# Starting the exit code of VectorE and ScalarE on a fetch-block boundary, in a group-norm kernel bound by DMA

## Chip, cores, metric

One NeuronCore of a Trainium2 chip. The metric is the device time in microseconds (us) of one execution. An execution's *span*, from the first to the last of the program's own instructions, is recorded beside it. The time was about 2 us more than the span in every run (1.79 to 2.02 us in the means of the kernels); this difference, called *time minus span* below, is what this study turned out to be about. Spans are recorded to 0.1 us.

## The reference

```python
# x: (128, 1024, 32, 16) bf16; 32 groups of 32 channels x 512 pixels = 16384 values
xr = x.reshape(B, G, C // G, H, W)
mu = xr.mean(axis=(2, 3, 4), keepdims=True)
var = ((xr - mu) ** 2).mean(axis=(2, 3, 4), keepdims=True)
xn = (xr - mu) / jnp.sqrt(var + 1e-5)
return xn.reshape(B, C, H, W) * g[None, :, None, None] + b[None, :, None, None]
```

134 MB are read and 134 MB written.

## The kernel before

The input is cut into 32 pieces of 4 MB, each 128 partitions (4 samples x 32 groups) by 16384 values. A ring of six pieces lies in SBUF. TensorE and VectorE add up a piece, ScalarE squares it and takes the root, VectorE scales it in place, and SyncE issues loads and stores. ScalarE, TensorE and VectorE each run a loop on their own; the loop body stands in the program once (VectorE's closing branch, one source line, runs 32 times in the trace).

```python
def in_rounds(e, one, ahead=None):          # ScalarE, TensorE
    with nc.Fori(0, ROUNDS, 1, engines=[e.engine]) as t:
        more = (t, ahead(t)) if ahead else (t,)
        for c in range(REST):
            one(c, *more)
        with e.If(t < ROUNDS - 1):
            for c in range(REST, SLOTS):
                one(c, *more)

def on_vector(e):
    ...
    with nc.Fori(1, NT + 1, 1, engines=[e.engine]) as i:
        ...
        for k, a in enumerate(parts):       # 32 channels of a piece
            ts = e.tensor_scalar(
                out=a, in0=a, scalar1=scl[:, k : k + 1], scalar2=bia[:, k : k + 1],
                op0=ALU.mult, op1=ALU.add,
            )
            if (k + 1) % KQ == 0:
                ts.then_inc(done, 1)

def on_sync(e):
    ...                                     # all loads and stores of pieces
    e.wait_ge(s_fin, 16 * sum(store_parts(i) for i in range(NT - SLOTS, NT)))
```

When an engine leaves its loop, the *exit code* follows: on each engine a few drains and semaphore waits that form a closing barrier over all five engines (VectorE's first drain lasts 3.7 us, until its last scaling ends). Behind the barrier the trace names no instructions, but the device time of the profiled run, 630.24 us, is 2.0 us more than its span.

## Time and profile before

| | before |
|---|---|
| device time, median of the first 3 runs | 630.41 us (629.87 to 630.49) |
| span of the profiled run | 628.2 us |
| bytes moved, mean rate over the span | 268.44 MB, 427 GB/s |
| VectorE, ScalarE busy | 79%, 80% |
| last ScalarE, last VectorE arithmetic ends | 603.0, 614.3 us |
| last store lands, SyncE's wait ends | 627.6 us |

How to read it: the DMA engines are full until 622.5 us (busy share 1.00 from 620 to 622.5 us, 0.20 in the 2 us after), so the compute engines have slack, and everything that ScalarE and VectorE do after 603 and 614 us lies beside the last stores until 627.6 us. The busy times in part 1 of the page (us, share of the span, instructions):

```profile
PE 180.9 (29%) x513; PEld 0.2 (0%) x2; DVE 495.8 (79%) x1185; ACT 503.0 (80%) x258; POOL 1.0 (0%) x8
```

No compute engine is full. The prediction shows the other lines.

### The profile page before, as it was taken

To read this page: it belongs to the slowest core of one execution; us is meant where nothing else is said; L and a number is where in the kernel's file an instruction comes from. 1 tells how busy PE (TensorE), PEld (TensorE's weight loads), DVE (VectorE), ACT (ScalarE), POOL (GpSimd) and SP (SyncE) were. 2 spreads that over 40 slices of the span, in tenths; PEclk is the share of its full clock that TensorE was granted. 3 is DMA by queue.
4 is the path that set the end of the run, shared out by engine and by line. 5 is a ranking of instruction groups with operands and counts; after the bars stand their busy time and mean duration, and the time that the engine had idled before them with its cause. 6 is when DMAs were issued, how large, how long until landed. Compare 5 with 4: busy or idle time off the path is not lost.

```text
span 628.2 us, 2492 instructions
## 1 busy us (share of the span) xinstructions
PE 180.9 (29%) x513; PEld 0.2 (0%) x2; DVE 495.8 (79%) x1185; ACT 503.0 (80%) x258; POOL 1.0 (0%) x8
## 2 busy tenths in 40 slices
PE   2633334330244402333023330333303333063000
PEld 0000000000000000000000000000000000000000
DVE  1479999999298982999729997299973999799961
ACT  0899999999389992999919999199990999979930
POOL 0000000000000000000000000000000000000000
PEclk9776776675586655877558775577755776577555
DMA  9999999999999999999999999999999999999996
GB/s 401 434 434 401 434 434 434 434 434 434 432 434 434 434 434 434 432 432 430 434 434 434 432 426 434 434 432 432 434 430 432 430 432 434 432 432 434 434 434 275
DMA packets 9888, 268.44 MB, mean 427 GB/s; under 512 B 1184, under 2 KB 1184, under 8 KB 1184
## 3 DMA queue, kind: packets, MB, share of 16 engines
q1 hardware_dynamic: 9792, 268.44, 99.3%
q10 hardware_dynamic: 96, 0.00, 0.0%
HBM read 134.22 MB, written 134.22 MB: 427 GB/s over the span
## 4 chain that ended last, share of the span: by engine, by line
DMA 35%; ACT 35%; DVE 21%; PE 4%; issue 1%; DVEq 1%; SPq 0%; ACTq 0%
ACT ja L269 32%; DMA ring<-in_x_dram 23%; DVE ring L336 15%; DMA out_dram<-ring 11%; DVE jp L306 5%; PE ps L218 4%; DMA gb_b<-in_b_dram 2%; ACT jm L261 2%; ACT var L279 1%; ACT std L283 1%; DVEq L320 1%; DVE bia L330 0%; DVE scl L326 0%; DVE rstd L324 0%; SPq L170 0%
## 5 line engine op out<-in xcount | busy, mean ns | idle before, releaser
L269 ACT ACTIVATE ja<-ring,nm 128x8192 fp8e5<-128x8192 bf16 x64 | 455.8, 7122 | 2.1
L336 DVE TENSOR_SCALAR ring<-ring,scl,bia x1024 | 333.6, 407 | 1.2
L218 PE MATMUL ps<-ring,eye 128*128 128x512 bf16 x512 | 180.6, 525 | 394.0 <-DVE jp L306 227.3
L306 DVE SCALAR_TENSOR_TENSOR jp<-ring 128x4096 fp8e5 (+1 forms) x32 | 141.4, 4420 | 75.7 <-PE ps L218 75.7
L261 ACT ACTIVATE jm<-ps 128x513 fp8e5<-128x513 f32 x32 | 19.1, 597 | 94.1 <-PE ps L218 94.0
L324 DVE RECIPROCAL rstd<-std 128x1 f32 x32 | 5.5, 171 | 26.8 <-ACT std L283 25.8
L269 ACT ACTIVATION_READ_ACCUMULATOR ja<-ring,nm 128x1 f32 x64 | 11.9, 186 | 0.0
L279 ACT ACTIVATE var<-sq,eps_t 128x1 f32<-128x1 f32 x32 | 9.4, 295 | 1.0
L283 ACT ACTIVATE std<-sq,var 128x1 f32<-128x1 f32 x32 | 9.4, 294 | 1.0
L312 DVE COPY gb<-gb_p 128x64 f32<-128x64 f32 x1 | 0.2, 224 | 12.6 <-PE gb_p L213 12.6
L330 DVE SCALAR_TENSOR_TENSOR bia<-scl,nm,gb 128x32 f32<-128x32 f32 x32 | 8.0, 251 | 1.1
L326 DVE TENSOR_SCALAR scl<-gb,rstd 128x32 f32<-128x32 f32 x32 | 7.7, 241 | 1.1
L261 ACT ACTIVATION_READ_ACCUMULATOR jm<-ps 128x1 f32 x32 | 6.2, 194 | 0.0
L306 DVE DVE_READ_ACCUMULATOR jp<-ring (+1 forms) x32 | 4.5, 141 | 0.0
L213 PE MATMUL gb_p<-gb_b,rep 32*128 32x64 bf16 x1 | 0.2, 205 | 12.3 <-DMA gb_b<-in_b_dram 12.3
L257 ACT ACT_TABLE_LOAD x1 | 1.3, 1283 | 1.8 <-PEq L369 1.8
L194 POOL TENSOR_SCALAR_AFFINE_SELECT rep<-ones_b 32x128 bf16<-32x128 bf16 x1 | 0.3, 303 | 0.0
L190 POOL TENSOR_SCALAR_AFFINE_SELECT eye<-ones_b 128x128 bf16<-128x128 bf16 x1 | 0.3, 292 | 0.2 <-issue 0.2
L257 ACT ACTIVATE warm<-eps_t 128x1 f32<-128x1 f32 x1 | 0.2, 202 | 0.0
L186 POOL MEMSET ones_b<- 128x128 bf16 x1 | 0.2, 204 | 0.3 <-POOLq L369 0.3
L215 PEld LDWEIGHTS <-eye 128*128 128x128 bf16 x1 | 0.1, 105 | 0.1
L213 PEld LDWEIGHTS gb_p<-gb_b,rep 32*128 32x128 bf16 x1 | 0.1, 100 | 12.3 <-issue 12.3
(5 smaller groups left out, 0.5 us busy)
## 6 DMA issues: line engine op xcount, KB each, us to landing
ring<-in_x_dram SPq DMA_DIRECT2D x32, 4096.0 KB, 37.3
out_dram<-ring SPq DMA_DIRECT2D x30, 4096.0 KB, 27.8
out_dram<-ring SPq DMA_DIRECT2D x2, 2048.0 KB, 12.9
out_dram<-ring SPq DMA_DIRECT2D x4, 1024.0 KB, 11.4
gb_b<-in_g_dram ACTq DMA_DIRECT2D x1, 2.0 KB, 7.7
gb_b<-in_b_dram ACTq DMA_DIRECT2D x1, 2.0 KB, 11.0
```

Of the source, the lines that this page charges most:

```text
L218: return e.add_instruction(mybir.InstMatmult(name=nc.get_next_instruction_name(), engine=e.engine, start_tensor_calc=(k == 0), stop_tensor ...
L257: e.activation(out=warm[:], in_=eps_t[:], func=ACT.Sqrt)
L261: e.activation(out=jm[:], in_=sums_and_pairs(c), func=ACT.Identity, scale=-inv_n, accum_out=nm[:, place(c) : place(c) + 1], saturate=False ...
L269: e.activation(out=ja[:], in_=slot(c)[:, h * (F // 2) : (h + 1) * (F // 2)], func=ACT.Square, bias=nm[:, place(c) : place(c) + 1], scale=1 ...
L279: e.activation(out=var[:], in_=sq[:, 0:1], func=ACT.Identity, bias=eps_t[:], scale=inv_n).then_inc(varred[c], 1)
L283: e.activation(out=std[:, place(c) : place(c) + 1], in_=sq[:, 1:2], func=ACT.Sqrt, bias=var[:], scale=inv_n).then_inc(stded, 1)
L306: e.scalar_tensor_tensor(out=jp[:], in0=aps[0], scalar=1.0, in1=aps[1], op0=ALU.mult, op1=ALU.add, accum_out=aps[2], saturate=False,).then ...
L320: e.keepalive_nop([e.lower_ap(a) for a in (*parts, nm_i, std_i, *ahead)])
L324: e.reciprocal(out=rstd[:], in_=std_i).then_inc(inverted, 1)
L326: e.tensor_scalar(out=scl[:], in0=gb[:, 0:KC], scalar1=rstd[:], scalar2=None, op0=ALU.mult).then_inc(scaled, 1)
L330: e.scalar_tensor_tensor(out=bia[:], in0=scl[:], scalar=nm_i, in1=gb[:, KC : 2 * KC], op0=ALU.mult, op1=ALU.add,).then_inc(shifted, 1)
L336: ts = e.tensor_scalar(out=a, in0=a, scalar1=scl[:, k : k + 1], scalar2=bia[:, k : k + 1], op0=ALU.mult, op1=ALU.add,)
```

## The change

The intent: the exit code is to start a block of 128 instructions of its own, in the hope that what follows it is then fetched while the engine idles beside the last stores, not after the closing barrier. The block of 128 is the change's premise. The traces show instruction packets of 8192 bytes (in the kernel before at 629.54 and 630.04 us), not how many instructions these hold. A *slot* is an instruction's place in its block, counted from 0. The loader leaves a gap behind the loop and puts a branch over it (in the changed kernel 38 ns on ScalarE, 47 ns on VectorE). This is the whole diff:

```diff
+FETCH = 128
@@
+    def enter_exit(e):
+
+        e.addr_align(FETCH, max_nops=0)
+
@@ on_scalar
         in_rounds(e, one)
+        enter_exit(e)
@@ on_vector
                     ts.then_inc(done, 1)
+        enter_exit(e)
```

## The prediction

> **What bounds the kernel now.** I read the page first, because it says whether any engine is full. Parts 1 to 3 do, and the two lines below from part 2 and part 3 carry it.
>
> ```profile
> DMA  9999999999999999999999999999999999999996
> GB/s 401 434 434 401 434 434 434 434 434 434 432 434 434 434 434 434 432 432 430 434 434 434 432 426 434 434 432 432 434 430 432 430 432 434 432 432 434 434 434 275
> ...
> q1 hardware_dynamic: 9792, 268.44, 99.3%
> ```
>
> The 16 DMA engines are at nine tenths or more in every slice but the last, at a flat 434 GB/s. 268.44 MB at 434 GB/s is 618.5 us, so about 98% of the 628.2 us span is moving each byte in once and out once. VectorE is busy 79% and ScalarE 80%, so neither sets the pace. The chain of part 4 walks through ScalarE squares and VectorE scaling, but only because a store waits for them; with the queue never empty, that chain isn't the bound. No change of VectorE or ScalarE code inside the loop should move the middle of the run. What can move is the last slice.
>
> Second, the timeline of the last 29 us, since the change touches only code behind the loops.
>
> ```profile
> 602.74 0.29 ACT L283 ACTIVATE std<-sq,var 128x1 f32<-128x1 f32 x1
> 603.07 0.16 DVE L324 RECIPROCAL rstd<-std 128x1 f32 x1 [5.10 <-ACT std L283]
> ...
> 603.83 10.42 DVE L336 TENSOR_SCALAR ring<-ring,scl,bia  x32
> 606.54 8.08 SPq L170 DMA_DIRECT2D out_dram<-ring  x4
> ```
>
> ScalarE's last activation ends at 603.03 us, VectorE's last at 603.83 + 10.42 = 614.25, and the last store is issued by 614.62. From there only DMA works: 13.6 us until the span ends at 628.2. The waits of the store queue say so too:
>
> ```profile
> SPq L183 <- DMA out_dram<-ring: 12.9, 1, 12.9
> ```
>
> This is the kernel's one wait for its last stores: 12.9 us long. ScalarE stands about 24.5 us and VectorE about 13 us at the closing barrier.
>
> Third, the exit code itself: the instructions of the closing barrier, which the profile lists under one line of the launch code.
>
> ```profile
> L380 ACTq DRAIN  x2: 8/12/15, 603.1 to 627.9; - x2
> L380 DVEq DRAIN  x2: 19/1868/3717, 610.6 to 628.0; - x2
> L380 SPq EVENT_SEMAPHORE  x2: 17/17/17, 627.9 to 628.2; - x2
> L380 ACTq EVENT_SEMAPHORE  x2: 17/17/17, 627.9 to 628.2; - x2
> L380 DVEq EVENT_SEMAPHORE  x2: 21/21/21, 627.9 to 628.2; - x2
> ```
>
> The exit code per engine is short: two drains and two semaphore waits. ScalarE reaches its first drain at 603.1 us, 0.1 us after leaving its loop, VectorE at 610.6 us (its sequencer is ahead of its arithmetic by ten queued operations). Neither shows a stall on entering the exit, so in the kernel before the exit code was already in instruction memory. The last two waits end at 628.2: that is the end of the span.
>
> Fourth, the DMA view of stretches that the page leaves out: 628 to 632 us, after the kernel's own code.
>
> ```profile
> DMA packets 2, 0.02 MB, mean 4 GB/s; under 512 B 0, under 2 KB 0, under 8 KB 0
> ...
> q14 instruction: 2, 0.02, 1.1%
> ```
>
> Two packets of the instruction kind, 8192 bytes each, start at 629.54 and 630.04 us in the trace and take 0.31 and 0.40 us. The same view of 0 to 628 us has queues 1 and 10 alone, so no instructions at all were fetched while the kernel ran. [...] So right after the closing barrier somebody runs into code that isn't there. Also, the profiled run took 630.24 us by the device's count and its span is 628.2: 2.0 us of the count lie outside the span, and these fetches end at 629.85 and 630.44, 1.6 and 2.2 us behind it.
>
> [...] the VectorE compare-and-branch at the loop's end took 50 ns here[...].
>
> **The change, part by part.** It adds one alignment mark behind each of the two loops, with no padding executed: the loader leaves a gap and branches over it. (1) Added: one branch per engine, 0.05 us, at 603.0 and 610.5 us. Both lie beside the stores; on the path to the end: 0. (2) Moved: [...] I expect the two packets of 629.5 and 630.0 to move to about 603 and 611 us. If the fetch is a cold one, the time is some 1.3 us (end of the code, 628.2, to the first packet, 629.5) plus 0.3 to 0.4 us of packet, say 1.7 us idle; between stores I allow three times that, 5 us. ScalarE has 24.5 us to spare and VectorE, which needs nothing new before 627.9, 17 us from 610.6. VectorE's ten queued operations run on meanwhile. On the path: 0. (3) Added to the stores' DMA: two packets of 8 KB among 268 MB. On one DMA engine each costs 0.3 to 0.4 us. The end is set by the slowest of 16 engines: in the trace 15 of the last 16 completions land by 625.1 and the last at 627.56. Only if a fetch falls on that one engine does the end move, by up to 0.4 each; 1 in 16 if spread evenly. Expected: under 0.05 us. (4) Removed: the wait after 628.2. If the two engines stall there for their code, the count holds up to 1.7 to 2.2 us of it[...]. I take 0.5 to 1 us as what must remain, hence a gain of 1.0 to 1.5 us where the fetch is inside the count. Sum where it is: 630.4 - 1.25 = 629.2. Sum where it isn't: 630.4.
>
> **The rivals.** First, the fetches are outside the count or are mere prefetches that nobody waits for. For it: the second one ends at 630.44, later than 630.24, and a prefetch would look the same; against it: two packets match the two engines that the author picked, and a start of the count some tenths before the first instruction would be enough to explain the 630.24. It makes 630.4, no change. I give it 40%. Second, the fetch collides with the last stores, on the engine that lags by 2.4 us, or slows VectorE before it has issued its last scaling. For it: the DMA engines are full until 622.5 us; against it: 16 KB only, and the queued VectorE work. It makes 630.7 to 631.2; 7%. Third, the marks shift the loops[...]: at 1.7 us for each of 31 VectorE back edges that is 53 us of VectorE time, of which its 21% of idle time (132 us) could hide most, but late stores would make 640 and more. Against it: the marks stand behind the loops, and the loop bodies (VectorE 48 recorded instructions, ScalarE eight per sample and six samples) are short; 1%. The main view, a real gain of about 1.25 us, has the remaining 52%.
>
> **Range and chances.** 0.52 x 629.2 + 0.40 x 630.4 + 0.07 x 630.9 + 0.01 x 640 = 629.9; I lean to the likeliest case and put 629.6. The three runs of before spread over 0.62 us, so I widen the two main cases by 0.5 either way and cut at the bottom for a gain of nearly 2 us: 628.4 to 630.9. Two per cent would be 12.6 us, six times all that lies outside the span, and nothing in the loop changes: faster by 2% 0.005, slower by 2% 0.01, within 0.985.
>
> **What would show each step.** Right: instruction packets of 8 KB inside the span near 603 and 611 us, none or fewer after 628; a span that stays at 628.2 within 0.5 us; ScalarE's and VectorE's first drain up to 5 us later than 603.1 and 610.6; count minus span down from 2.0 to 0.5 to 1.0 us. If the packets move and count minus span stays at 2.0, the first rival holds. If the span grows with the last store's completion later, the second. If instruction packets appear all through the span, the third. If the packets stay at 629.5 and 630.0, they belonged to other engines, and step (2) is wrong.

What the prediction told of the hardware and no trace or run of this case showed is cut from it, and the cuts are marked: a paragraph of rules and figures for instruction fetches and branches (the 50 ns of VectorE's compare-and-branch stay, from the trace), the size of an instruction, the reason given in step (2) for the packets to move, the reason given in step (4) for a rest that must remain, and in the third rival how a back edge would come to fetch. The sum came to 630.4 - 1.25 = 629.2 us where the fetch is inside the count and 630.4 where it isn't, and weighted with the rivals to 629.9, put as 629.6. The 0.5 to 1 us that must remain was from no measured number. The third rival's 53 us, 31 times 1.7, assumed a back edge that fetches anew in each turn, which had not been shown.

## The result

The changed kernel took 630.41 us (median of 6 runs, 630.14 to 630.97), the kernel before 630.40 us (6 runs). The ratio is 1.0003, 95% interval 0.999 to 1.0016: the same. Ratios here are the mean time of one kernel's fast runs over that of the other's of the same rounds, so not quite the ratio of the medians.

The span of the profiled run is 628.2 us, as before. The DMA part of the page of the changed kernel:

```profile
GB/s 401 432 434 403 434 434 434 434 434 432 434 434 432 434 430 432 434 432 434 434 434 434 434 434 430 432 432 428 434 432 434 430 430 430 432 426 434 434 435 286
DMA packets 9890, 268.46 MB, mean 427 GB/s; under 512 B 1184, under 2 KB 1184, under 8 KB 1184
...
q14 instruction: 2, 0.02, 0.0%
```

The rates are those of before. New is the row of queue 14: two instruction packets inside the span. In the trace they start at 607.80 and 615.51 us. The wait of SyncE for the last stores, and the exit code (one source line, by engine and kind: shortest/median/longest in ns, then the first and last start in us):

```profile
SPq L185 <- DMA out_dram<-ring: 12.4, 1, 12.4
```

```profile
L388 ACTq DRAIN  x2: 8/48/88, 604.0 to 627.9; - x2
L388 DVEq DRAIN  x2: 19/1605/3191, 611.6 to 627.9; - x2
L388 SPq EVENT_SEMAPHORE  x2: 17/17/17, 627.8 to 628.1; - x2
L388 ACTq EVENT_SEMAPHORE  x2: 17/17/17, 627.8 to 628.1; - x2
L388 DVEq EVENT_SEMAPHORE  x2: 21/21/21, 627.8 to 628.2; - x2
```

and the branches that the loader put in:

```profile
L214 ACTq COMPARE_BRANCH  x1: 38/38/38, 603.6 to 603.6; - x1
L214 DVEq COMPARE_BRANCH  x1: 47/47/47, 611.1 to 611.1; - x1
```

By the trace ScalarE's branch ends at 603.59 and its first drain starts at 603.98: 0.39 us for entering the block. On VectorE it is 611.13 to 611.63: 0.50 us. In the kernel before, the step from the loop's last branch to the first drain was 0.04 and 0.05 us. Both engines then stand at the barrier until 627.8 us, so these delays cost nothing. Behind the end, the DMA view of 628 to 632 us shows one packet where there were two:

```profile
DMA packets 1, 0.01 MB, mean 2 GB/s; under 512 B 0, under 2 KB 0, under 8 KB 0
...
q14 instruction: 1, 0.01, 0.9%
```

So the fetch moved, in part, and the time did not. Three questions follow. Whose are the packets? Did anyone wait for them? What would a real wait cost?

### The profile page after: what moved, and what is told of

It is laid out like the page before. It is cut to its first block, busy times and chain, and to the rows that moved or that the text cites. A ratio compares the mean times of both kernels' runs of the same rounds, so it can differ in the third digit from the quotient of the medians.

```text
span 628.2 us, 2489 instructions
## 1 busy us (share of the span) xinstructions
PE 187.3 (30%) x508; PEld 0.2 (0%) x2; DVE 495.9 (79%) x1185; ACT 503.0 (80%) x258; POOL 1.0 (0%) x8
## 4 chain that ended last, share of the span: by engine, by line
DMA 35%; ACT 35%; DVE 20%; PE 5%; issue 1%; DVEq 1%; SPq 0%; ACTq 0%
ACT ja L275 32%; DMA ring<-in_x_dram 23%; DVE ring L343 15%; DMA out_dram<-ring 11%; PE ps L224 5%; DVE jp L313 4%; DMA gb_b<-in_b_dram 2%; ACT jm L267 2%; ACT var L285 1%; ACT std L289 1%; DVEq L327 1%; DVE bia L337 0%; DVE scl L333 0%; DVE rstd L331 0%; SPq L172 0%
## 5 line engine op out<-in xcount | busy, mean ns | idle before, releaser
L224 PE MATMUL ps<-ring,eye 128*128 128x512 bf16 x507 | 187.1, 542 | 387.8 <-DVE jp L313 221.7
```

The costliest lines, as they stand in the source:

```text
L224: return e.add_instruction(mybir.InstMatmult(name=nc.get_next_instruction_name(), engine=e.engine, start_tensor_calc=(k == 0), stop_tensor ...
```

## The experiments

Theory A: the packets behind the end were prefetches (fetches made ahead of need) of a next block, asked for when an engine ran into a block that it already had; no one waited. Theory B: an engine did wait, and the gain was lost again in the stores. Every experiment was run five times, each beside runs of the kernel before on the same chip, and every kernel gave the right result.

### r1_before_again and r2_after_again: both kernels, with the span of every run

No edit.

> The kernel before once more, for the span of each of its runs, which decides what a change of the count is made of. Theory A (the fetches behind the end are prefetches that no one waits for): count minus span about 1.9 us, the same as in the changed kernel within 0.1 us; two 8 KB instruction packets 1.2 to 1.9 us behind the end of the span, none inside it. Theory B (the engines wait for these fetches, and what the change saved was lost again in the stores): count minus span here at least 0.4 us above the changed kernel's, and its span shorter by as much.

> The changed kernel once more beside it. Both theories: ratio 1.000 within 0.001, instruction packets near 608 and 615 us and one about 1.7 us behind the end. Theory A: count minus span within 0.1 us of the kernel before. Theory B: count minus span lower by 0.4 us or more, span longer by as much.

Measured: 630.56 and 630.17 us (medians); ratios to the runs of before 1.0000 (0.9986 to 1.0013) and 0.9995 (0.9981 to 1.0009). Behind the end of the span r1 has packets at +1.02 and +1.80 us, r2 one at +1.68. Over all runs:

| kernel | runs | time minus span, mean and standard error | span, mean and its range |
|---|---|---|---|
| before | 31 | 2.02 ± 0.01 us | 628.5 us (627.9 to 629.3) |
| changed | 11 | 1.86 ± 0.02 us | 628.5 us (628.1 to 629.1) |

The change saved 0.17 us behind the span, by these means. That is 0.03% of the time and a small part of the 1.4 us by which spans of the kernel before differ among themselves. The mean span is unchanged, so theory B's second half falls: nothing was lost in the stores, at least nothing over the 0.25 us to which the two means can be compared. Its first half falls too, as far as the device time goes, for it needed 0.4 us.

### r3_scalar_only and r4_vector_only: one mark each

Against the changed kernel, r3 and then r4:

```diff
                     ts.then_inc(done, 1)       # on_vector
-        enter_exit(e)
```

```diff
         in_rounds(e, one)                      # on_scalar
-        enter_exit(e)
```

> The mark on ScalarE alone. If the packets inside the span belong one to each engine: one packet, near 608 us. If the two packets behind the end in the kernel before were those of ScalarE and VectorE: one of them stays, near 629.5 to 630. If the packet that the changed kernel still has behind the end is a third engine's, there are two behind the end here. Time: the same within 0.1% by both theories A and B (B: up to 0.5 us less if ScalarE's fetch was the one that ended last).

> The mark on VectorE alone. One packet inside the span, near 615 us, about 4.4 us after VectorE leaves its loop at 611. Behind the end as many as with the mark on ScalarE alone if the two engines are alike. Time: the same within 0.1% by theory A; by B up to 0.5 us less if VectorE's fetch was the one that ended last.

Measured: 630.39 and 630.49 us, ratios 1.0001 (0.9987 to 1.0015) and 0.9999 (0.9986 to 1.0013). Each has one packet inside the span, at 607.92 us (ScalarE) and 614.96 us (VectorE). Behind the end, r3 first, then r4, in the DMA view of 628 to 633 us:

```profile
q14 instruction: 1, 0.01, 0.4%
```

```profile
q14 instruction: 2, 0.02, 1.2%
```

ScalarE's mark takes one of the two packets away; VectorE's takes none. The two packets of before were not the two marked engines': only one was, ScalarE's, and in the trace the one that goes is the earlier. VectorE's mark added a fetch during the stores and removed nothing. Time minus span says the same: 1.87 ± 0.01 us with ScalarE's mark, 1.98 ± 0.03 with VectorE's, against 2.02.

### r5_all_five: marks on every engine

```diff
 # on SyncE ahead of the last wait; on TensorE behind its loop; on GpSimd behind its last op
+        enter_exit(e)
         e.wait_ge(s_fin, 16 * sum(store_parts(i) for i in range(NT - SLOTS, NT)))
```

> Marks on all five engines, SyncE's ahead of its last wait. By the runs so far, count minus span is 2.02 us in the kernel before (14 runs), 1.86 in the changed one (11), 1.87 with ScalarE's mark alone and 1.98 with VectorE's: one of the two packets behind the end was ScalarE's, none VectorE's, and one still stands at 1.7 us behind the end. Theory A (a third engine owns it, and it is a prefetch): no instruction packet within 2 us behind the end, five inside the span or in the seconds of idle engines, count minus span 1.7 to 1.86. Theory A2 (it belongs to the runtime's own code far behind ours): the packet stays. Theory B (an engine waits for it): count minus span falls by 0.5 us or more.

Measured: 630.91 us, ratio 1.0001 (0.9988 to 1.0015). It was run on another chip. No packet stands behind the end, in the view of 628 to 633 us:

```profile
DMA packets 0, 0.00 MB, mean 0 GB/s; under 512 B 0, under 2 KB 0, under 8 KB 0
```

The view of 0 to 628 us has five inside:

```profile
q14 instruction: 4, 0.03, 0.0%
...
q8 instruction: 1, 0.02, 0.0%
```

By their times and the engines' exits: GpSimd's at 5.45 us, ScalarE's at 607.80, VectorE's at 615.51, SyncE's at 618.94, these four of 8192 bytes each, and one of 16384 bytes on queue 8 at 592.44 us, which must be TensorE's, the only mark left. Time minus span is 1.79 ± 0.02 us: against the changed kernel's 1.86 that is 0.06 ± 0.03 us less, hardly clear of noise. So the remaining packet was a third engine's, and inside the device time almost no one waited for it.

### r6_sync_last and r7_sync_last_two: the entry on the path to the end

```diff
         e.wait_ge(s_fin, 16 * sum(store_parts(i) for i in range(NT - SLOTS, NT)))
+        enter_exit(e)
# and none on ScalarE and VectorE; r7: a nop and a second mark behind it
```

> One mark alone, on SyncE behind its wait for the last stores: the entry into an aligned block lies on the path to the end. Entry took 0.38 us on ScalarE and 0.50 us on VectorE in the changed kernel, from the end of the branch to the first drain. If that is a cost of any entry: the span grows by 0.4 to 0.5 us against the kernel before of the same rounds, with the drain of SyncE later behind its wait by as much. If the target had to be fetched: 1.3 to 2 us.

> The same with two marks, one idle instruction between them: the second branch goes into a block whose prefetch began only when the first block was entered, 0.1 us earlier. The packets behind the end began 1.0 to 1.3 us after the code that asked for them and took 0.3 to 0.5, so a real wait for a fetch is to cost 1.3 to 2 us here, and the span grows by 1.8 to 2.5 us in all. If it grows by 1.0 us or less, two blocks or more are held ahead.

Measured: r6 630.98 us, ratio 1.0003 (0.9989 to 1.0016), r7 630.97 us, 1.0001 (0.9987 to 1.0014). They were run on another chip. r7 failed as an experiment: its idle instruction fell away, only one branch ran, and it is a second r6. In both, SyncE's branch ends 0.40 us before its next drain (627.82 to 628.22 in r6, 627.92 to 628.32 in r7). Mean spans are 628.98 and 628.90 us, 0.3 and 0.2 us above the 628.70 of the kernel before in these rounds, so less than the 0.4 to 0.5 us expected, but spans of five runs are only good to about 0.2. The packet that came with the branch started 0.97 us after it, at 628.79, and the late packet of before at about +1.8 us is gone. That one was SyncE's. SyncE ran its next drain before the packet started: a prefetch. Time minus span is 1.99 ± 0.01 us in both.

### r8_sync_last_124: a boundary in the middle of the closing barrier

```diff
         e.wait_ge(s_fin, 16 * sum(store_parts(i) for i in range(NT - SLOTS, NT)))
+        e.addr_align(FETCH, offset=124, max_nops=0)
# and none on ScalarE and VectorE
```

> The mark on SyncE behind its last wait, but four instructions short of the block's end: the next block is asked for 0.6 us before it is needed, and SyncE runs into it right behind the closing barrier. If the count holds what the engines do behind the span: count minus span grows by 0.4 to 1.5 us over 2.02, or the span does where the crossing falls into the closing barrier. If the count ends with the closing barrier and a fixed allowance: count minus span stays at 2.0.

Measured: 630.74 us, ratio 1.0000 (0.9986 to 1.0013). It was run on another chip. SyncE has five instructions of exit code, so by blocks of 128 the last of them is the first in the next block:

```profile
L387 SPq EVENT_SEMAPHORE  x2: 17/17/17, 628.4 to 628.9; - x2
L387 ACTq EVENT_SEMAPHORE  x2: 17/17/17, 628.4 to 628.7; - x2
```

Without the crossing, SyncE's last wait starts 5 ns before ScalarE's (r1: 628.114 and 628.119). Here it comes at 628.876 against 628.697: **running over a block boundary into a block already held cost SyncE 0.18 us** (one trace). That the delay falls on this instruction agrees with blocks of 128. The next packet starts 0.63 us after it, at 629.51. The expectation was wrong: there was no fetch to wait for, the branch itself took only 0.12 us and no packet followed it, so slot 124 evidently lay in the block SyncE was in. Time minus span went down, not up, to 1.86 ± 0.02 us. The span grew at its very end by 0.14 us: SyncE's last wait ends at 628.89, and TensorE's, which ends the span in the kernel before, at 628.76. That is about what time minus span lost, so the device time did not follow SyncE's delay. That what the other engines do after 628.70 sets its end instead is argued, not shown.

### r9_sync_two_hops: a real wait for a fetch

```diff
         e.wait_ge(s_fin, 16 * sum(store_parts(i) for i in range(NT - SLOTS, NT)))
+        enter_exit(e)
+        e.drain()
+        enter_exit(e)
# and none on ScalarE and VectorE
```

> SyncE behind its last wait enters an aligned block, runs one drain there and branches into the next block, asked for at most half a microsecond before (r7 was to do this, but its idle instruction fell away and only one branch ran). The first entry cost 0.40 us in r6 and r7. Theory A, that the changed kernel never waited for a fetch: this is what such a wait looks like, 1.3 to 2 us between the second branch and the next drain, and the span grows by 1.8 to 2.5 us against the kernel before. If the second entry costs 0.4 us as well, the block was there and this chip holds more ahead than the packets suggest.

Measured: 632.99 us against 630.21, ratio 1.0043 (1.0028 to 1.0057). Mean span 630.94 against 628.35: 2.6 us longer, a little more than expected. The branches, the drain between them, and the drains behind them, in three source lines' views:

```profile
L217 SPq COMPARE_BRANCH  x2: 33/33/33, 627.4 to 628.0; - x2
```

```profile
L187 SPq DRAIN  x1: 62/62/62, 627.9 to 627.9; - x1
```

```profile
L389 SPq DRAIN  x3: 7/7/58, 630.2 to 630.5; - x3
```

The first entry, 627.48 to 627.88, cost 0.40 us; the second, 628.04 to 630.16, cost 2.13. **This is what a wait for instructions looks like**, and it shows at full size in span and time. No such gap stands in the exit code of the kernel before or of the changed one, and behind the end, where the trace names no instructions, the whole time minus span, 2.02 us, is shorter than one such wait. The trace shows one thing more: SyncE went on only 1.14 us after the packet had landed (629.02 to 630.16; in r11, 1.2 to 1.3 us). The packets of the kernel before landed 1.60 and 2.19 us behind the end. As an estimate from these figures, a wait for either would have ended 2.7 us or more behind the end, while the device time reaches at most 2.02 us behind it if it starts no later than the span. Such a wait could then not have been saved from the device time; whether anyone waited outside it, these runs can't tell.

### r10_scalar_122: ScalarE's boundary put back behind the end

```diff
         in_rounds(e, one)
-        enter_exit(e)
+        e.addr_align(FETCH, offset=122, max_nops=0)
# and none on VectorE
```

> ScalarE's mark as in the change, but at slot 122 of a block in place of 0: branch and fetch as before, and four own instructions later the boundary comes again right behind the end of the span. In r8 SyncE's run over a boundary cost 0.18 us (its last wait ended at 628.88, the others' at 628.70). Theory A (what the change saved is ScalarE's crossing of a boundary, some 0.16 us of the count): count minus span is back at 2.0 us, 0.15 above r3. If the 0.16 us came of the branch or of the earlier fetch: it stays at 1.87.

Measured: 630.43 us, ratio 1.0003 (0.9989 to 1.0017). ScalarE branched at 604.2 us (packet at 609.09), and two packets stand behind the end again, at +1.31 and +1.68 us. Time minus span is 1.90 ± 0.04 us: 0.03 above r3, 0.12 below the kernel before. Inconclusive, and against theory A's simple form, which expected 2.0. A crossing behind the end did not by itself bring the 0.15 us back; it may matter at which instruction of the closing code it falls, which the trace doesn't show. Four instructions from slot 122 end at slot 125, so by blocks of 128 it lay here two unnamed instructions behind the end, not right behind it; where it lay in the kernel before is not known.

### r11_scalar_four_hops: five fetches among the last stores

```diff
         in_rounds(e, one)
         enter_exit(e)
+        e.drain(); enter_exit(e)      # three times, and a last drain
```

> The changed kernel with four hops of ScalarE over four blocks in place of one: does a fetch wait between the last stores, and do five fetches there delay the end? Theory A: each later hop waits for its fetch, 4 to 4.5 us as in the traces so far (branch at 603, packet at 607.8), so ScalarE is at its last drain at 616 to 619 us, 9 us ahead of the closing barrier; span and time as in the changed kernel within 0.2 us. The rival that fetches delay the stores: the span 0.3 to 1.2 us longer.

Measured: 630.35 us, ratio 0.9999 (0.9985 to 1.0013), mean span 628.40 us against 628.35. ScalarE's hops, the branches and the closing drain:

```profile
L214 ACTq COMPARE_BRANCH  x4: 33/36/38, 603.2 to 615.0; - x4
```

```profile
L395 ACTq DRAIN  x2: 8/8/8, 620.1 to 628.1; - x2
```

The first entry cost 0.39 us, the later three 5.7, 5.2 and 4.9 us each (branch end to next drain), slower than the 4 to 4.5 expected, and 2.3 to 2.7 times the 2.13 us of r9 with idle DMA engines. ScalarE was still 8 us early. Five instruction packets among the last stores moved the end by nothing that these runs resolve.

### r12_loop_over_edge: VectorE's loop laid across a boundary

```diff
-        with nc.Fori(1, NT + 1, 1, engines=[e.engine]) as i:
+        with nc.Fori(1, NT + 1, 1, engines=[e.engine], head_slot={e.engine: 100}) as i:
# no marks
```

> No mark at the exit; VectorE's loop is placed at slot 100 of a block, so that its body runs over a boundary in each of 32 turns. The third rival of the prediction, priced: if a back edge over a boundary fetched anew, 31 or more packets inside the span and up to 53 us of VectorE time. If both blocks stay: no packet inside the span, 0.15 to 0.5 us per turn on VectorE's sequencer, 5 to 16 us in all, most of it hidden under its queued scaling, and the time the same within 0.3%.

Measured: 630.61 us, ratio 1.0001 (0.9987 to 1.0016). One packet inside the span, at 38.4 us, in the first turn; none in the 31 turns after it:

```profile
q14 instruction: 1, 0.01, 0.0%
```

In the trace, from the loop's closing branch to the next register instruction the median is 0.23 us, against 0.14 in r1. So the two neighbouring blocks were both kept: one packet in 32 turns. A back edge between them cost 0.09 us of VectorE's sequencer, which is ahead of its arithmetic anyway (in the kernel before it reaches its first drain at 610.6 us, 3.7 us before the last scaling ends).

## Why the prediction was right and where it was wrong

The time, 630.41 us, lies in the range, and "within 2%" came true. But the point, 629.6, was 0.8 us low, and the case given the larger share (52%) was the wrong one. The range held both main cases, so that the time lies in it says nothing for the mechanism.

- **The bound** was read rightly: flat DMA at 434 GB/s, exit code of both engines hidden. r11 strengthens it: 17 us of ScalarE's exit (603 to 620) cost nothing.
- **Step 1**, the branches: 0.05 us was too little. With the step to the next instruction the entry costs 0.39 and 0.50 us. Still none of it on the path; r6 shows 0.40 us where it is.
- **Step 2**, the packets move inside the span: right for the inside, at 607.8 and 615.5 us, some 4 us after the branches. Entering was not cold: in r6 SyncE's next drain started 0.40 us after the branch, and the packet only 0.97 us after it. So what was fetched was not the block entered. That it was the block behind it agrees with r9, where the branch into that next block was the one that waited, 2.13 us. Wrong about ownership: "two packets match the two engines" was a coincidence. One was ScalarE's (r3), the other SyncE's (r5, r6), and VectorE had none to move.
- **Step 3**, the stores' DMA: right. Mean spans are equal within their noise of 0.25 us, and r11's five packets cost nothing.
- **Step 4**, the wait after 628.2, is the step that failed. It took a packet behind the end for a wait of 1.7 to 2.2 us and expected a gain of 1.0 to 1.5. The gain is 0.17 us. A real wait was measured in r9 at 2.13 us, with 1.14 us of it after the packet had landed, so by that estimate a wait for these packets would have ended too late to lie in the device time. The 0.5 to 1 us that "must remain" rested on no number; 1.86 remain. The fourth view read the two packets as "somebody runs into code that isn't there", which no line there shows. Under its first rival the prediction did note that a prefetch would look the same, but it weighed the count of two packets more.
- **The first rival** (40%: prefetches that nobody waits for) is what happened, but for the 0.17 us. That the packets are prefetches is shown where SyncE ran on before its packet started (r6, r8); for ScalarE's packet behind the end it is argued from these. The rival's other wording, fetches outside the count, is not needed and not excluded. **The second** is refuted by the spans. **The third** is refuted by the changed kernel's two packets, where a fetch in each turn would show many, and in r12 a loop over two neighbouring blocks was harmless (ratio 1.0001); one that leaves both was not tried.
- **What the 0.17 us is.** Shown: it belongs to ScalarE's mark. Time minus span is 1.79 to 1.90 us in every kernel with a mark on ScalarE (r11: 1.83 ± 0.03) and 1.98 to 2.02 in every other (r9 2.01, r12 1.98) but r8, whose span grew at its end. And running over a boundary cost SyncE's sequencer 0.18 us even though the block was there (r8). That ScalarE's own crossing right behind the end is this 0.17 us was argued from the two numbers; r10, made to show it, returned only 0.03 of it, with the boundary two instructions further on. That stays open.

## What to carry to other kernels

A fetch packet in the trace need not be a wait (in r6 SyncE's next drain started 0.57 us before the packet): look for a gap between two instructions of the sequencer that would have waited. Here a real one was 2.1 us (r9), 4.9 to 5.7 us among heavy DMA traffic (r11), and entering a block that was already there 0.18 us (r8, running on) to 0.50 us (the changed kernel's VectorE, by a branch). The packet itself started 4.2 to 4.9 us after the branch that set it off among the stores (the changed kernel, r10), against 0.97 us with idle DMA engines (r6). Before moving something off the end of a kernel, find out whose it is by moving one engine's at a time. An engine that idled beside the last transfers could be given 17 us more to do at its exit without the time moving (r11); a wait on the engine that waits for the last transfer moved it by its full size (r9).
